# Unsplit fp32 matmuls for the first operands of a two-pass DFT kernel, with another order of its first accumulations

## The chip, the cores and the metric

The kernel runs on one core of one Trainium2 chip. The metric is the device time of one execution in microseconds (us). TensorE (PE) multiplies, VectorE (DVE), ScalarE (ACT) and GpSimd (POOL) work beside it, and SyncE (SP) and POOL each issue transfers from a queue of their own. Inputs lie in HBM.

## What is computed

```python
xn = layernorm(x)                       # x: 2048 x 640
a, b = xn @ hid_re.T, xn @ hid_im.T     # DFT along the hidden dimension
s = seq_re @ a - seq_im @ b             # DFT along the sequence, real part
g = silu(((silu(xn @ w_gate) * (xn @ w_up)) @ w_down))
out = x + s * g
```

Everything is float32. The kernel takes the sequence DFT first (`seq @ xn`), then the hidden one.

## The kernel before, in words

**Precision.** A float32 operand is split into two fp32r parts, `high` and `low`: ACT writes high (L192), DVE writes low = value - high (L197, or L199 where a factor of -1 is folded in). A product is three matmuls, high x high, high x low, low x high (`mm3`, L213 to L215), each 128x128 by 128x512.

**Tiling.** `seq(k)` is called four times (real and imaginary part of the sequence DFT for two halves of its columns). Each call is one level of a Strassen-like scheme with the products p1, d, p5, p2, p6, p3, p7, p4 in this order for k = 0. A product runs over four quarters g = 0..3; a quarter holds two tiles kk of 128 contraction rows. A quarter of p1 has, for each of its tiles, two matmul groups into the banks of p1 and one `direct` group for the last 128 of the 640 columns: 18 matmuls. A quarter of d has the direct group alone (6 matmuls), one of p5, p6, p3 or p7 two groups (12), one of p2 three (18).

**Left operands** come from the DFT matrix `cs`, 128x1024 float32 a quarter (512 KB): Y[g] is block 11, R[g] block 21. `load` (L569) issues them from SP. `accumulate` (L583) adds another block onto the tile in SBUF by a transfer that adds, from POOL: R[g] becomes a21 + a22 after d (`d`, L703), is read by p5, then gets block 11 added (`p5`, L697) and is read by p6 (`p6`, L716). An accumulation must wait until the split that reads the old value is done; the next split waits until it has landed.

**Right operands** are the normalized x. `layer_norm` (L413) works on two tiles of x: DVE statistics (L420, L422), a chain of small operations on DVE (L433 to L437, after a square root on ACT, L432), for tiles 8 to 15 on POOL instead (L441 to L448), and the rows are applied by ACT (L453). Then `right_operand` (L604) splits them, one, two or four tiles at once.

**Order.** `Plan` gives every operation a due time: matmul steps follow each other at 0.226 us a matmul, what they need is due some lead (`LEAD`, L540) before its step, and all operations are sorted by due time (L73). This settles only the order within each engine's and queue's program and where buffers lie; on the chip each engine runs its own list in order, as soon as semaphores allow. Before the first product, 22 matmuls of zeros run (`busy`, L457, called at L1050), and 6 more stand ahead of the third quarter of p1 (L661). The matmuls of p1 and d for k = 0 are interleaved: p1 quarters 0 and 1, d quarter 0, p1 quarter 2, d 1, p1 3, d 2, d 3 (L734).

Of the kernel before, what the change touches and what calls it, by code (L numbers as in the profile page):

```python
# [10 lines left out]
AF = mybir.ActivationFunctionType  # L11
ALU = mybir.AluOpType

P = 128
S, D, F = 2048, 640, 1536
TC = 512
# [121 lines left out]
def tile_fnet_swiglu(  # L138
# [34 lines left out]
    def raw(name, a=0, n=None):  # L173
        o = where[name]
        return raw_arena[:, o + a:o + (pl.size[name][1] if n is None else a + n)]

    def hl(name, i, a=0, n=None):

        key = name, "hl"[i]
        o = where[key]  # L180
        return hl_arena[:, o + a:o + (pl.size[key][1] if n is None else a + n)]


    def split(lead, dst, n, src, reads, a=0, scale=None, sub=0, low_lead=None):


        def like(ap):
            s = src()
            return ap.rearrange("p (a b) -> p a b", b=s.shape[2]) if len(s.shape) == 3 else ap

        def high():
            nc.scalar.activation(like(hl(dst, 0, a, n)), src(), AF.Copy, scale=1.0 if scale is None else scale)  # L192

        def low():
            hi, lo = like(hl(dst, 0, a, n)).bitcast(F32), like(hl(dst, 1, a, n))
            if scale is None:
                nc.vector.tensor_tensor(lo, src(), hi, op=ALU.subtract)  # L197
            else:
                nc.vector.scalar_tensor_tensor(lo, src(), scale, hi, op0=ALU.mult, op1=ALU.subtract)  # L199

        pl.prod(lead, high, reads, [(dst, "h", sub)])
        pl.prod(lead - 2 if low_lead is None else low_lead, low, [*reads, (dst, "h", sub)], [(dst, "l", sub)])

    def both(dst, *subs):
        return [(dst, p, s) for s in (subs or (0,)) for p in "hl"]
# [4 lines left out]
    def mm3(bank, w, m, first, a=0, n=TC):  # L210

        o = ps[:, bank, a:a + n]
        nc.tensor.matmul(o, w(0), m(0), start=first, stop=False, skip_group_check=True)  # L213
        nc.tensor.matmul(o, w(0), m(1), start=False, stop=False, skip_group_check=True)  # L214
        nc.tensor.matmul(o, w(1), m(0), start=False, stop=True, skip_group_check=True)  # L215

    def product(todo, reads):

        banks = sorted({t[0] for t in todo})

        def go():
            for bank, w, m, first in todo:
                mm3(bank, w, m, first)

        pl.step(3 * len(todo), go, reads, [("ps", b) for b in banks])

    def pair(b):
        return ps[:, b[0]:b[0] + len(b), :]
# [276 lines left out]
    def down_operands():  # L505

        for g in range(2):
# [29 lines left out]
    spare = down_operands()  # L537


    LEAD = {("xn", 0): ((2.6, 1.0), (6, 6), (7, 7)), ("xn", 1): ((3.9, 2.0), (4.31, 4.22), (6.2, 4.32)),  # L540
# [10 lines left out]

    def seq(k):
        j, ri = k // 2, k % 2
# [2 lines left out]
        first = {}  # L556
        top, made = {}, set()
        fresh = k == 0

        def is_first(b):  # L560
            f = first.setdefault(b, True)
# [27 lines left out]
                    [(src, 0)], [(dst, 0)])  # L589

        def operand(p, g, name):
            s = pl.buf(("S", k, p, g), "hl", 4 * TC)
            high, low = LEAD.get((p, g), LEAD.get(p, LEAD["S"])) if fresh else LEAD["S"]
            for i, sub in enumerate(halves(p, g)):
                n = 2 * TC // len(halves(p, g))
                lead = (high, low) if n > TC else LEAD["S", i]
                split(lead[0], s, n, lambda i=i, n=n: raw(name, i * n, n), [(name, j) for j in range(2) if n > TC or j == i],
                      i * n, sub=sub, low_lead=lead[1])
            return s

        def halves(p, g):
            return (0, 1) if fresh and (p, g) == ("p1", 0) else (0,)

        def right_operand(p, g, per):  # L604

# [17 lines left out]
        def run(*parts, order=None):  # L623

            todo = []
            start = pl.now
            for i, g in order or [(0, g) for g in range(4)]:  # L630
                p, left, banks, direct = parts[i]
                rights = ([p] if banks else []) + ([f"d{direct[1]}"] if direct else [])
                per = 3 * (len(banks) + (direct is not None))
                at = pl.now
                s = left(g)
                for kk in (2 * g, 2 * g + 1):
                    pl.now = at + kk % 2 * per * MM
                    for r in rights:
                        few = 4 if not fresh or r not in ("p1", "d1", "p2", "d2") else 2 if g > 2 or r[1] == "2" else 1
                        if (r, kk) not in top:  # L640
                            right_operand(r, kk // few, few)
                pl.now = at + 2 * per * MM
                todo.append((p, g, banks, direct, rights, s))
            pl.now = start
            for p, g, banks, direct, rights, s in todo:
                steps = [], []
                reads = [], []
                for kk in (2 * g, 2 * g + 1):
                    i = kk % 2
                    m = lambda part, i=i, s=s: hl(s, part, i * TC, TC)  # L650
# [4 lines left out]
                    subs = halves(p, g)  # L655
                    reads[i].extend(both(s, subs[i % len(subs)]))
                    for r in rights:
                        reads[i].extend(both(*top[r, kk][:2]))
                if fresh and p == "p1":
                    if g == 2:  # L660
                        pl.step(0, lambda: busy(ps[:, b1[0]], 6), [], [("ps", b1[0])])  # L661
                    for step in zip(steps, reads):
                        product(*step)
                else:
                    product(steps[0] + steps[1], list(dict.fromkeys(reads[0] + reads[1])))

        def result(q, b, other, op):
            name = pl.buf(("P", k, q), "raw", len(b) * TC)
# [18 lines left out]
        def p1(g):  # L687
            if not fresh:
                Y[g] = load(11, g, 18)
                return operand("p1", g, Y[g])  # L690
            for i in range(2):
                load_x(2 * g + i, 30 + (3.9 if g == 1 else 0), nc.sync)
            Y[g] = load(11, g, 30) if g else load_tiles(11, (30, 29.8))
            layer_norm(2 * g, 2, *LEAD["xn", g], nc.vector)
            return operand("p1", g, Y[g])
# [7 lines left out]
        def d(g):  # L703
            R[g] = load(21, g, 26 if fresh else 18)
            s = operand("d", g, R[g])
            accumulate(R[g], 22, g, LEAD["d", g][1] - 0.1 if fresh else 7.5)
            return s

        def p2(g):
            if fresh:  # L710
                for kk in (8 + 2 * g, 9 + 2 * g):
                    load_x(kk, (32, 32.7, 31.7, 35.8)[g], nc.gpsimd if g else nc.sync)
                layer_norm(8 + 2 * g, 2, *LEAD["xn", 4 + g], nc.gpsimd)
            return operand("p2", g, load(12, g, 14 if fresh else 17))

        def p6(g):  # L716
            if not fresh:
# [21 lines left out]
            run(first_two[1])  # L739
        if not fresh:  # L740
            product_2()
        run(("p5", p5, b3, None))
        n5 = copy("n5", b3)
        if fresh:
            product_2()
# [346 lines left out]
```

## Time and profile before

| | |
|---|---|
| median of 3 runs | 996.8 us (996.42 to 998.02) |
| the profiled execution | 996.99 us, span 994.6 us from first to last instruction |
| PE, weight loads, DVE, ACT, POOL busy | 99%, 81%, 72%, 50%, 11% |
| mean granted TensorE clock | 0.998 |
| HBM read, written | 145.75 MB, 33.57 MB |

How to read it: PE is busy nearly all the time, so what can be had lies in the moments in which it isn't. The profile names for each wait of an engine the instruction that ended it. A matmul row shows its latency (0.39 us); consecutive ones start 0.227 us apart, and a larger step between two starts is a wait or a slower clock. A row of the timeline may merge equal neighbours: `x3` and the time from the first start to the last end. Queue instructions that issue transfers show only the issue; when data has landed is seen from the engine that waited.

### The profile page before, as it was taken

What the parts mean: (1) busy time and instruction counts of PE and PEld (TensorE: products, weight loads), DVE (VectorE), ACT (ScalarE), POOL (GpSimd) and SP (SyncE); (2) the same over time, 40 slices, a digit from 0 to 9 for tenths busy, and PEclk for the clock granted to TensorE, in tenths of its full rate; (3) what the DMA queues carried; (4) which work ended last, traced back from release to release, by engine and by line L of the source; (5) the groups of instructions that cost most, each with busy time, mean ns of one, the idle gap of its engine ahead of it and who ended that gap; (6) DMA issues with size and microseconds to landing.
All of it is one profiled execution on the core that took longest, in us unless ns stands there. A gap on an engine that the chain in (4) does not pass through costs nothing.

```text
span 994.6 us, 11790 instructions
## 1 busy us (share of the span) xinstructions
PE 982.2 (99%) x4317; PEld 806.2 (81%) x4318; DVE 714.5 (72%) x935; ACT 500.8 (50%) x718; POOL 107.7 (11%) x175
## 2 busy tenths in 40 slices
PE   8999999999999999999999999999999999999998
PEld 5777888888888888888888888888888888887887
DVE  7979767856686686466678886787677666666686
ACT  6676553754375454414655555444334544444342
POOL 1650201011102010001111110000010100000000
PEclk9999999999999999999999999999999999999999
DMA  9779667565756586643535645679950311115683
GB/s 337 213 171 266 225 144 161 209 193 136 179 190 202 134 227 217 216 163 133 186 122 195 229 164 175 205 236 361 323 186 27 106 54 53 53 43 172 230 276 133
DMA packets 71466, 180.10 MB, mean 181 GB/s; under 512 B 6448, under 2 KB 22064, under 8 KB 71408
## 3 DMA queue, kind: packets, MB, share of 16 engines
q1 hardware_dynamic: 57072, 125.71, 38.2%
q0 software_dynamic: 14336, 53.63, 19.5%
q8 instruction: 34, 0.56, 0.2%
q14 instruction: 24, 0.20, 0.1%
HBM read 145.75 MB, written 33.57 MB: 180 GB/s over the span
## 4 chain that ended last, share of the span: by engine, by line
PE 90%; DVE 4%; DMA 3%; ACT 1%; issue 1%; POOL 1%; DVEq 0%; ACTq 0%; POOLq 0%
PE ps L213 30%; PE ps L214 30%; PE ps L215 30%; DMA raw<-in_cs 2%; DVE hl L197 2%; ACT hl L192 1%; DVE bst L420 0%; ACT raw L453 0%; DVE raw L477 0%; DMA raw<-in_x 0%; DVE raw L588 0%; DVE raw L243 0%; POOL raw L585 0%; POOL sm L441 0%; POOL sm L442 0%
## 5 line engine op out<-in xcount | busy, mean ns | idle before, releaser
L213 PE MATMUL ps<-hl 128*128 128x512 f32 (+1 forms) x1430 | 556.7, 389 | 2.9 <-ACT hl L192 2.0
L215 PE MATMUL ps<-hl 128*128 128x512 f32 (+1 forms) x1430 | 556.2, 389 | 2.6 <-DVE hl L197 1.5
L214 PE MATMUL ps<-hl 128*128 128x512 f32 (+1 forms) x1430 | 556.0, 389 | 0.4 <-DVE hl L197 0.4
L192 ACT ACTIVATE hl<-raw 128x1024 fp32r<-128x1024 f32 (+7 forms) x511 | 376.5, 785 | 250.6 <-DVE raw L875 52.5
L197 DVE TENSOR_TENSOR hl<-raw,hl 128x1024 fp32r<-128x1024 f32 (+5 forms) x438 | 395.2, 934 | 131.6 <-ACT hl L192 88.3
L213 PEld LDWEIGHTS ps<-hl 128*128 128x128 f32 x1430 | 268.8, 188 | 60.6 <-ACT hl L192 3.0
L215 PEld LDWEIGHTS ps<-hl 128*128 128x128 f32 x1430 | 268.8, 188 | 59.6 <-DVE hl L197 2.4
L214 PEld LDWEIGHTS ps<-hl 128*128 128x128 f32 x1430 | 268.9, 188 | 56.7 <-DVE hl L197 1.6
L238 ACT ACTIVATE raw<-ps 128x512 f32<-128x512 f32 (+1 forms) x122 | 80.3, 676 | 145.5 <-PE ps L215 107.8
L243 DVE TENSOR_TENSOR raw<-ps,raw 128x512 f32<-128x512 f32 (+1 forms) x90 | 71.6, 796 | 54.2 <-PE ps L215 53.3
L962 DVE TENSOR_TENSOR raw<-raw 128x512 f32<-128x512 f32 x24 | 16.6, 692 | 49.8 <-ACT raw L961 49.8
L199 DVE SCALAR_TENSOR_TENSOR hl<-raw,hl 128x384 fp32r<-128x384 f32 (+5 forms) x73 | 43.8, 601 | 7.8 <-ACT hl L192 4.4
L875 DVE TENSOR_TENSOR raw<-raw 128x256 f32<-128x256 f32 (+1 forms) x96 | 47.8, 519 | 0.0
L585 POOL DMA_DIRECT2D raw<-in_cs x36 | 32.2, 1070 | 128.5 <-DVE raw L588 91.4
L588 DVE TENSOR_TENSOR raw<-raw 128x1024 f32<-128x1024 f32 x28 | 34.1, 1219 | 9.8 <-DMA raw<-in_cs 9.8
L1024 POOL DMA_DIRECT2D out<-raw x10 | 6.7, 673 | 303.1 <-ACT hl L192 245.7
L676 POOL DMA_DIRECT2D p_dram<-raw x24 | 17.2, 760 | 202.3 <-DVE raw L243 153.6
L828 DVE TENSOR_TENSOR raw<-raw 128x1024 f32<-128x1024 f32 (+1 forms) x24 | 24.0, 1040 | 6.4 <-DMA raw<-in_xt 6.4
L940 ACT ACTIVATE raw<-raw 128x512 f32<-128x512 f32 x24 | 15.2, 632 | 23.6 <-DVE raw L243 23.5
L800 POOL DMA_DIRECT2D y_dram<-raw x20 | 10.9, 547 | 132.4 <-ACT raw L238 132.4
L961 ACT ACTIVATE raw<-ps 128x512 f32<-128x512 f32 x24 | 14.3, 596 | 19.7 <-PE ps L215 18.7
L532 POOL DMA_DIRECT2D d_p<-hl x28 | 15.2, 542 | 79.6 <-ACT hl L192 65.5
(45 smaller groups left out, 186.3 us busy)
## 6 DMA issues: line engine op xcount, KB each, us to landing
raw<-in_cs SPq DMA_DIRECT2D x79, 512.0 KB, 5.8
hl<-d_p SPq DMA_DIRECT2D x56, 384.0 KB, 4.1
raw<-in_cs POOLq DMA_DIRECT2D x36, 512.0 KB, 8.9
raw<-in_wb SPq DMA_DIRECT2D x24, 640.0 KB, 4.0
d_p<-hl POOLq DMA_DIRECT2D x28, 384.0 KB, 2.8
raw<-p_dram SPq DMA_DIRECT2D x8, 1280.0 KB, 9.8
p_dram<-raw POOLq DMA_DIRECT2D x16, 512.0 KB, 6.5
raw<-in_hd SPq DMA_DIRECT2D x20, 320.0 KB, 9.0
```

Of the source, the lines that this page charges most:

```text
L192: nc.scalar.activation(like(hl(dst, 0, a, n)), src(), AF.Copy, scale=1.0 if scale is None else scale)
L197: nc.vector.tensor_tensor(lo, src(), hi, op=ALU.subtract)
L199: nc.vector.scalar_tensor_tensor(lo, src(), scale, hi, op0=ALU.mult, op1=ALU.subtract)
L213: nc.tensor.matmul(o, w(0), m(0), start=first, stop=False, skip_group_check=True)
L214: nc.tensor.matmul(o, w(0), m(1), start=False, stop=False, skip_group_check=True)
L215: nc.tensor.matmul(o, w(1), m(0), start=False, stop=True, skip_group_check=True)
L238: pl.post(lambda: nc.scalar.activation(wide(raw(dst, a, n)), pair(b), AF.Copy), pkeys(b), [(dst, a)], after)
L243: pl.post(lambda: nc.vector.tensor_tensor(wide(raw(dst, a, n)), pair(b), wide(raw(other)), op=op), [*pkeys(b), (other, 0)], [(dst, a)], after)
L585: pl.prod(lead, lambda: nc.gpsimd.dma_start(wide(raw(name)), source(q, g), accum_op=ALU.add), [], [(name, 0), (name, 1)], 8)
L588: pl.prod(lead, lambda: nc.vector.tensor_tensor(raw(dst), raw(dst), raw(src), op=ALU.add), [(src, 0)], [(dst, 0)])
L828: pl.prod(46 - 6 * q - 2 * i - half, lambda i=i, op=op, part=part, rows=rows, nb=nb: nc.vector.tensor_tensor(part(), part(), raw(rows, i * ...
L875: pl.prod(lead, lambda o=o, a=a, b=b, op=op: nc.vector.tensor_tensor(o(), a(), b(), op=op), [(w, 0)], [(c, lead)])
```

## The change

- Quarter 0 of p1 and quarters 0 and 1 of d (k = 0) are no longer split. Each of their products is one `nc.tensor.matmul` on float32 operands: 6 in p1 quarter 0, 2 in each of the two d quarters. Since p1 takes minus x, ACT writes a negated copy of 256 columns of tiles 0 and 1 (`negative`). `halves`, which split p1's first operand by tile, goes away.
- The accumulations onto R[0] and R[1] are now planned right behind the d matmuls that read R itself, and wait for these (before, for the low parts).
- The 6 matmuls of zeros ahead of p1's third quarter are removed.
- p5 takes its quarters in the order 0, 2, 3, 1. p6 keeps 0, 1, 2, 3.
- Leads: the rows of tiles 2 and 3 and of tiles 8 to 11 and 14, 15 are applied by other due times; loads of x tiles 10 to 15 and of p2's blocks are due later; the second pair of x tiles is issued behind both halves of p1's first block.

What this makes of each list: POOL's transfers stood before as accumulation on R[0], x 10, 11, accumulation on R[1], x 12 to 15, accumulations on R[2], R[3]; they now stand as R[0], x 10, 11, R[2], R[3], R[1], x 12 to 15. The second round, block 11 onto R, stood as R[0], (small operations for tiles 14, 15), R[1], R[2], R[3]; it now stands as R[0], (the same), R[2], R[3], R[1]. From p3 on the lists of PE, ACT and DVE are the same as before.

```diff
-            for bank, w, m, first in todo:
-                mm3(bank, w, m, first)
-        pl.step(3 * len(todo), go, reads, [("ps", b) for b in banks])
+            for bank, w, m, first, *unsplit in todo:
+                if unsplit:
+                    nc.tensor.matmul(ps[:, bank, :], w(), m(), start=first, stop=True, skip_group_check=True)
+                else:
+                    mm3(bank, w, m, first)
+        pl.step(sum(4 if len(t) > 4 else 3 for t in todo), go, reads, [("ps", b) for b in banks])
...
+        whole = {("p1", 0), ("d", 0), ("d", 1)} if fresh else ()
...
         def operand(p, g, name):
+            if (p, g) in whole:
+                return name
...
-        def halves(p, g):
-            return (0, 1) if fresh and (p, g) == ("p1", 0) else (0,)
+        def negative(kk):
+            name = pl.buf(("neg", kk), "raw", 256)
+            pl.prod(LEAD["neg", kk], lambda: nc.scalar.activation(
+                raw(name).unsqueeze(1), xn_tiles(kk, 1, 0, 256), AF.Copy, scale=-1.0), [(xn, kk, 0)], [(name, 0)])
+            return name
...
+                    if (p, g) in whole:
+                        m = lambda i=i, s=s: raw(s, i * TC, TC)
+                        for e, b in enumerate(banks):
+                            steps[i].append((b, lambda n=top["neg", kk], e=e: raw(n, e * P, P), m, is_first(b), True))
+                        w = lambda kk=kk: xn_tiles(kk, 1, TC, P)[:, 0]
+                        steps[i].append((dbank[direct[0]], w, m, is_first(dbank[direct[0]]), True))
+                        reads[i].extend([(s, i), (xn, kk, 0)] + ([(top["neg", kk], 0)] if banks else []))
+                        continue
...
-                    if g == 2:
-                        pl.step(0, lambda: busy(ps[:, b1[0]], 6), [], [("ps", b1[0])])
...
+                if p == "d" and (p, g) in whole:
+                    accumulate(R[g], 22, g, 0)
...
-                load_x(2 * g + i, 30 + (3.9 if g == 1 else 0), nc.sync)
+                load_x(2 * g + i, 30 + (5.2 if g == 1 else 0), nc.sync)
...
-            accumulate(R[g], 22, g, LEAD["d", g][1] - 0.1 if fresh else 7.5)
+            if ("d", g) not in whole:
+                accumulate(R[g], 22, g, LEAD["d", g][1] - 0.1 if fresh else 7.5)
...
-                    load_x(kk, (32, 32.7, 31.7, 35.8)[g], nc.gpsimd if g else nc.sync)
+                    load_x(kk, (32, 27.5, 25.4, 29.4)[g], nc.gpsimd if g else nc.sync)
...
-            return operand("p2", g, load(12, g, 14 if fresh else 17))
+            return operand("p2", g, load(12, g, 11 if fresh else 17))
...
-        run(("p5", p5, b3, None))
+        run(("p5", p5, b3, None), order=((0, 0), (0, 2), (0, 3), (0, 1)) if fresh else None)
```

More of the change, by code (lines that the diff above doesn't have):

```diff
@@ L537, in tile_fnet_swiglu @@
     spare = down_operands()
-    LEAD = {("xn", 0): ((2.6, 1.0), (6, 6), (7, 7)), ("xn", 1): ((3.9, 2.0), (4.31, 4.22), (6.2, 4.32)),
[6 rows of a table removed]
+    LEAD = {("xn", 0): ((2.6, 1.0), (6, 6), (7, 7)), ("xn", 1): ((4.1, 3.1), (6.4, 6.3), (7.5, 6.5)),
+            ("xn", 2): ((3.9, 3), (5, 4.5), (6.8, 6.1)), ("xn", 3): ((3.9, 3), (6.87, 6.7), (9.8, 7.9)), ("xn", 4): ((11, 11), (17, 17), (17.1, 17.1)),
+            ("xn", 5): ((10, 10), (18.1, 18.1), (18.2, 18.2)), ("xn", 6): ((7.5, 7.5), (15.7, 15.7), (15.8, 15.8)),
+            ("xn", 7): ((7.5, 7.5), (15.4, 15.4), (15.5, 15.5)), ("neg", 0): 1.8, ("neg", 1): 2.6,
[1 row of a table added]
             ("Tp1", 4): (0, 3.8, 2.6), ("Td1", 4): (0, 3.7, 2.55), ("Tp1", 5): (0, 4.9, 3.5), ("Td1", 5): (0, 4.8, 3.4),
[3 rows of a table removed]
[4 rows of a table added]
     def seq(k):
@@ L591, in operand @@
         def operand(p, g, name):
+            if (p, g) in whole:
+                return name
             s = pl.buf(("S", k, p, g), "hl", 4 * TC)
             high, low = LEAD.get((p, g), LEAD.get(p, LEAD["S"])) if fresh else LEAD["S"]
[L594 to L598, printed above, removed]
-            return s
-        def halves(p, g):
-            return (0, 1) if fresh and (p, g) == ("p1", 0) else (0,)
+            split(high, s, 2 * TC, lambda: raw(name), [(name, 0), (name, 1)], low_lead=low)
+            return s
+        def negative(kk):
[3 more added lines that the diff above has]
+            return name
         def right_operand(p, g, per):
@@ L632, in run @@
                 rights = ([p] if banks else []) + ([f"d{direct[1]}"] if direct else [])
-                per = 3 * (len(banks) + (direct is not None))
+                per = (4 if (p, g) in whole else 3) * (len(banks) + (direct is not None))
                 at = pl.now
@@ L637, in run @@
                     pl.now = at + kk % 2 * per * MM
+                    if (p, g) in whole:
+                        if p == "p1":
+                            top["neg", kk] = negative(kk)
+                        continue
                     for r in rights:
@@ L649, in run @@
                     i = kk % 2
+                    if (p, g) in whole:
+                        m = lambda i=i, s=s: raw(s, i * TC, TC)
[4 more added lines that the diff above has]
+                        reads[i].extend([(s, i), (xn, kk, 0)] + ([(top["neg", kk], 0)] if banks else []))
+                        continue
                     m = lambda part, i=i, s=s: hl(s, part, i * TC, TC)
@@ L654, in run @@
                         steps[i].append((dbank[direct[0]], tw(rights[-1], kk, 0), m, is_first(dbank[direct[0]])))
-                    subs = halves(p, g)
-                    reads[i].extend(both(s, subs[i % len(subs)]))
+                    reads[i].extend(both(s))
                     for r in rights:
```

14 rows, old and new, of the table LEAD are left out of this document.

## The prediction, made before the changed kernel ran

> **What bounds the kernel now.** The page first, then stretches of the span, then PE's starts in order of time.
>
> ```profile
> PE 982.2 (99%) x4317; PEld 806.2 (81%) x4318; DVE 714.5 (72%) x935; ACT 500.8 (50%) x718; POOL 107.7 (11%) x175
> ```
> ```profile
> 9.00:107.00 98.00, 92.91 (x391) 73.02 (x390) 88.10 (x134) 67.10 (x87) 32.66 (x53) 0.98 0.85 253
> 107.00:986.00 879.00, 878.19 (x3880) 726.76 (x3880) 619.40 (x784) 428.79 (x623) 74.23 (x115) 1.00 0.55 173
> ```
>
> From 107 us on PE misses 0.8 us in 879: there only matmuls count, 0.2265 us each (879/3880), and the change leaves them alone. (Buffers are placed anew, so that a write may meet another reader; the 0.8 us bounds such waits as they are now, and I take none.) Everything it can win or lose lies in the first 107 us, and it counts only if the last wait there, at 107 us, ends earlier or later. PE's waits:
>
> ```profile
> 12.82 0.50 PE L215 MATMUL ps<-hl 128*128 128x512 f32 x1 [0.70 <-DVE hl L199]
> ...
> 20.25 1.24 PE L460 MATMUL ps<-z 128*128 128x512 bf16 x5
> 22.17 0.50 PE L213 MATMUL ps<-hl 128*128 128x512 f32 x1 [0.68 <-ACT hl L192]
> ...
> 29.32 0.50 PE L213 MATMUL ps<-hl 128*128 128x512 f32 x1 [1.37 <-ACT hl L192]
> 29.67 0.40 PE L214 MATMUL ps<-hl 128*128 128x512 f32 x1
> 30.41 0.65 PE L215 MATMUL ps<-hl 128*128 128x512 f32 x1 [0.35 <-DVE hl L199]
> ...
> 51.80 0.50 PE L215 MATMUL ps<-hl 128*128 128x512 f32 x1 [1.37 <-DVE hl L197]
> 52.15 0.40 PE L213 MATMUL ps<-hl 128*128 128x512 f32 x1
> ...
> 85.21 0.50 PE L214 MATMUL ps<-hl 128*128 128x512 f32 x1 [0.39 <-DVE hl L197]
> ...
> 107.17 0.50 PE L213 MATMUL ps<-hl 128*128 128x512 f32 x1
> ```
>
> PE waits for splits, late because DVE and ACT are full (DVE 90% of this stretch), and behind them for the accumulations. The chain of waits has two long transfers, each followed by the split that needs it:
>
> ```profile
> 32.13 11.47 DMA raw<-in_cs
> 43.69 1.07 ACT hl L192
> ...
> 59.43 13.11 DMA raw<-in_cs
> 72.62 1.07 ACT hl L192
> ```
>
> The first is the last of the a22 accumulations, the second (issued 59.43, landed 72.54) the third of POOL's seven in a row:
>
> ```profile
> 58.26 6.26 POOL L585 DMA_DIRECT2D raw<-in_cs  x7 [0.28 <-ACT hl L192]
> ```
>
> **The change part by part.**
>
> *Unsplit matmuls.* No row shows one. Three matmuls leave out low x low, so four passes of 0.2265, 0.91 us, is my value: ten products, +2.3 us of PE. Bounds from the nearest rows: one pass each, -4.5 us in all; four passes at the slow clock's 0.43 us (below), +10.4. The Trainium skill, "FP8 and Floating Point Precision", section TensorE Precision Notes, gives true FP32 four passes; by that the sum is the same +2.3.
>
> *Splits removed.* Durations, grouped by form:
>
> ```profile
> L197 DVE TENSOR_TENSOR hl<-raw,hl 128x1024 fp32r<-128x1024 f32 x18 | 21.4, 1218 | 3.0 <-ACT hl L192 2.9
> L197 DVE TENSOR_TENSOR hl<-raw,hl 128x512 fp32r<-128x512 f32 x5 | 3.4, 678 | 0.2 <-ACT hl L192 0.2
> L199 DVE SCALAR_TENSOR_TENSOR hl<-raw,hl 128x256 fp32r<-128x256 f32 x6 | 2.4, 396 | 0.4 <-ACT hl L192 0.4
> L197 DVE TENSOR_TENSOR hl<-raw,hl 128x128 fp32r<-128x128 f32 x6 | 1.7, 284 | 0.0
> L192 ACT ACTIVATE hl<-raw 128x256 fp32r<-128x256 f32 x10 | 4.1, 412 | 0.2
> ```
>
> DVE loses two each of these four: 2 x (1.22 + 0.68 + 0.40 + 0.28) = 5.2 us. ACT loses the same high parts and gains two negations of 0.41. First product: tile 0's rows are applied as now,
>
> ```profile
> 7.29 0.92 ACT L453 ACTIVATE raw<-raw,sm,rowst 128x640 f32<-128x640 f32 x1 [0.50 <-DVE sm L437]
> ```
>
> so it is negated by 8.6, and the zeros end at 9.0: no new wait. The second pair of x tiles is issued one slot later; DVE has no split ahead of their statistics any more, which covers it. The earlier due times of rows cost nothing: ACT works 67 of these 98 us.
>
> *Zeros removed.* The wait of 20.25 to 22.17 was for tile 4's rows and splits; the DVE chain behind them ended at 20.7, three subtractions and one sum stood ahead of quarter 3's splits:
>
> ```profile
> 20.55 0.16 DVE L437 SCALAR_TENSOR_TENSOR sm<-mv,rowst 128x2 f32<-128x2 f32 x1
> ...
> 25.12 3.50 DVE L197 TENSOR_TENSOR hl<-raw,hl 128x1024 fp32r<-128x1024 f32 x3
> 28.54 1.22 DVE L477 TENSOR_TENSOR raw<-raw 128x1024 f32<-128x1024 f32 x1
> 29.67 0.69 DVE L199 SCALAR_TENSOR_TENSOR hl<-raw,hl 128x512 fp32r<-128x512 f32 x1
> ```
>
> Laid end to end in the new order, DVE has: statistics of tile 3 to 10.4, chain for 2, 3 to 11.6, p1 quarter 1 low (after its high) 12.0 to 13.2, tile 2 lows (after ACT) 14.0 to 14.6, statistics 4 to 15.7, tile 3 lows to 16.2, statistics 5 to 17.3, quarter 2 low to 18.4, chain for 4, 5 to 19.3: 1.4 us sooner, and tile 4's high part is there at 20.4 + 0.3. PE arrives at 9.0 + 6 x 0.91 + 18 x 0.2265 + 2 x 0.91 = 20.3: the wait shrinks to some 0.3. Quarter 2 and d 1 take it to 26.5. Quarter 3's low part comes after two subtractions instead of three, all 1.4 sooner: 2 x 1.15 + 1.2 + 0.7 from 23.8 is 28.0, where it was 30.4, and no slow clock follows a wait this short. So p5 begins at 28.0 + 28 x 0.2265 = 34.3; it began 20 slots after 33.85 (below), at 38.4.
>
> *Accumulations of a22.* R[0]'s now waits for PE's d 0 (20.3); x 10 and 11 queue behind it, uncritical. R[1]'s waits for d 1, but stands behind R[3]'s anyway. The four x tiles that stood ahead of the last two now follow: 4 x 320 KB at 405 GB/s is 3.2 us,
>
> ```profile
> 34.00:36.00 2.00, 2.00 (x11) 1.63 (x10) 1.93 (x7) 0.32 (x1) 0.00 (x0) 1.00 1.00 405
> ```
>
> and d's splits come about 1.5 us sooner. The last landing, at 43.6 in the chain, moves to about 38.9. p5's quarter 3 then meets its low part at about 40.8 (DVE has statistics between), 1 us of wait, and the last two quarters, p2 (72 matmuls) and p6's quarter 0 (12) follow without one: 40.8 + 108 x 0.2265 = 65.2. Before, p6 quarter 0 ended at 52.15 + 81 x 0.2265 = 70.5. The order 0, 2, 3, 1 does its work: **PE leads by 5.3 us** here.
>
> *Block 11 onto R, where the lead goes.* p6 still takes quarter 1 second, but R[1]'s accumulation is now third of POOL's row. When does that row begin? Behind POOL's small operations for tiles 14 and 15, which need DVE's statistics. In the new order DVE finishes R[1]'s low part at 38.9 + 1.06 + 0.9 + 1.2 = 42.0, then statistics 2.2, p2's splits 1.2 and 1.1, statistics 2.2: 48.5. POOL's eight operations took, by pair of tiles:
>
> ```profile
> 41.20:47.00 5.80, 5.15 (x8) 1.00 0.07 13
> 48.10:52.20 4.10, 3.52 (x8) 1.00 0.01 2
> ```
>
> Long beside DVE's back-to-back subtractions (three at 42.29 to 46.0), short between. Behind these statistics stands a run of subtractions again: 5.7 us, so the row begins at 54.3, 4.0 us before today's 58.26. Landings of the first three today, from what ACT waited for, and DVE behind them:
>
> ```profile
> 63.82 1.06 ACT L192 ACTIVATE hl<-raw 128x1024 fp32r<-128x1024 f32 x1 [0.22 <-DMA raw<-in_cs]
> 68.77 2.01 ACT L192 ACTIVATE hl<-raw 128x1024 fp32r<-128x1024 f32 x2 [3.90 <-DMA raw<-in_cs]
> ```
> ```profile
> 69.87 1.23 DVE L197 TENSOR_TENSOR hl<-raw,hl 128x1024 fp32r<-128x1024 f32 x1 [3.54 <-ACT hl L192]
> ```
>
> R[1] as third lands 72.54 - 58.26 = 14.3 after the row's start: 68.6. **PE stands from 65.2 to 69.7**, and to 70.9 for the low part. Behind that split on ACT and DVE queue quarters 2 and 3, whose data is there, and everything of p3.
>
> *What ends last.* DVE makes p6's quarter 1 low at 69.7 and quarter 2 low at 70.9; that one starts at 69.87 today. From there DVE's list is today's, nearly without a gap, down to the combination that frees PE's bank at 107.17:
>
> ```profile
> 105.90 1.22 DVE L243 TENSOR_TENSOR raw<-ps,raw 128x1024 f32<-128x1024 f32 x1
> ```
>
> So 36.0 us later again: 107.17 + 1.0. PE's own count agrees: quarter 1 at 70.9 against 70.7, plus a slow-clock window (1.7), less today's waits at 81.8, 85.2 and 107.2 (1.3): +0.6. The sum is **+1.0 us** on the profiled execution's 996.99 (span 994.6 and 2.4 around it): 998.0. The median of the runs is 0.2 below that execution, so 997.8.
>
> **The rivals.**
>
> *The lead survives.* If R[1]'s second accumulation lands by 64, PE keeps its 5.3 us at p6 and DVE's list gives up to 4.0 (the row's earlier start): 996.8 - 4.3 = 992.5. For it: 4 to 5 us less DVE work is real. Against: R[1] would have to land 10 us after its row starts, as second does today (68.77 - 58.26 = 10.5), and it is third.
>
> *It lands half-way.* POOL's pair takes 4.1 instead of 5.7, and p3's loads from SP, which share the queue's time with the first two, come later: 1.6 + 1 us sooner, 995.2.
>
> *The clock: slower.* Today's wait of 27.8 to 29.3 halves the clock afterwards:
>
> ```profile
> 30.00:32.00 2.00, 1.65 (x5) 1.30 (x5) 2.00 (x4) 2.00 (x3) 0.62 (x1) 0.65 1.07 316
> 32.00:34.00 2.00, 2.00 (x6) 1.51 (x6) 2.00 (x2) 0.42 (x1) 0.87 (x1) 0.50 1.05 272
> 33.42 0.63 PE L213 MATMUL ps<-hl 128*128 128x512 f32 x1
> 33.85 0.47 PE L214 MATMUL ps<-hl 128*128 128x512 f32 x1
> ```
>
> Eight matmuls 0.43 apart, 1.6 us lost. The new wait is three times as long. If it slows two such stretches once PE runs again, PE's count passes DVE's: +0.6 + 1.7 = +2.3, and with R[1] a microsecond later +3.3: 1000.1. It decides as soon as more than one stretch is slow behind 70.9. The Trainium skill, "TensorE: Matmul & The Clock Gate", section HAM oscillation, warns only of idle gaps over about 3.4 us; the trace is stricter, 1.5 and 0.5 us were enough, and by the page too the new gap of 4.5 is long enough. An unsplit product of 1.6 us instead of 0.91 would make PE 7 us later, use up the lead, and end near the same 1000.
>
> *The change does not do what it says* finds no support: the new lists hold the ten single matmuls, the negations and the transfers in the order told.
>
> **How the numbers follow.** About 0.2% (2 us) is what a measurement of this kernel can tell from none: faster is below 994.8, slower above 998.8. Forecast, 997.8 (996.0 to 999.3): 0.50. Half-way, 995.2: 0.17. Lead kept, 992.5: 0.13. Slow clock or dear matmuls, 1000.1: 0.20. Faster: 0.13 and 0.07 of half-way, 0.20. Slower: 0.20 and 0.12 of the forecast's upper end, 0.32. The range, 994.0 to 1000.4, leaves out the kept lead and a little on the other side.
>
> **What would show it.** The new page should have PE's longest wait near 65 to 70 us, ended by ACT L192 behind a transfer, a granted clock of about 0.5 soon after, no half clock near 31, PE's waits before p5 under 2 us in all, unsplit rows 0.91 us apart. Wrong, if POOL's row of seven begins before 52, if p6's second quarter starts before 67, or if PE is late at p6 (unsplit matmuls far from 0.91).

## The result, and the profile after

| | before | after |
|---|---|---|
| median of 22 runs each, in turn on the same chips | 996.8 us (996.36 to 998.02) | 998.8 us (997.49 to 1001.14) |
| the profiled execution, its span | 996.99, 994.6 us | 998.95, 997.0 us |

The ratio after : before is 1.0021, with a 95% interval of 1.0014 to 1.0028: 2.0 us slower. The forecast was 997.8.

First the page's line of busy times and two stretches of the changed kernel; columns of the stretches are length, PE, PEld, DVE, ACT, POOL busy, granted clock, DMA share, GB/s.

```profile
PE 982.7 (99%) x4302; PEld 804.2 (81%) x4302; DVE 710.5 (71%) x927; ACT 496.8 (50%) x712; POOL 106.2 (11%) x175
```
```profile
9.00:107.00 98.00, 91.07 (x363) 69.07 (x363) 83.42 (x128) 62.32 (x81) 31.29 (x53) 0.97 0.78 228
107.00:986.00 879.00, 878.25 (x3881) 726.69 (x3880) 620.22 (x783) 429.53 (x624) 73.35 (x114) 1.00 0.55 176
```

Behind 107 us nothing has changed (0.75 us without PE, 0.8 before). In the first 98 us DVE does 4.7 us less (83.42 for 88.10) and ACT 4.8 less, and still PE's missing time rises from 5.1 to 6.9 us. PE's starts in order of time; the number in brackets is the wait just before, with what ended it.

```profile
8.76 2.84 PE L224 MATMUL ps<-raw 128*128 128x512 f32 x6 [0.16 <-ACT raw L606]
12.07 2.84 PE L224 MATMUL ps<-raw 128*128 128x512 f32 x6 [0.47 <-ACT raw L606]
14.95 0.50 PE L213 MATMUL ps<-hl 128*128 128x512 f32 x1
...
21.54 0.50 PE L213 MATMUL ps<-hl 128*128 128x512 f32 x1 [0.46 <-ACT hl L192]
...
25.76 1.88 PE L224 MATMUL ps<-raw 128*128 128x512 f32 x4
27.74 0.50 PE L213 MATMUL ps<-hl 128*128 128x512 f32 x1
...
28.65 0.50 PE L215 MATMUL ps<-hl 128*128 128x512 f32 x1 [0.17 <-DVE hl L199]
...
65.22 0.39 PE L215 MATMUL ps<-hl 128*128 128x512 f32 x1
70.76 0.79 PE L213 MATMUL ps<-hl 128*128 128x512 f32 x1 [5.15 <-ACT hl L192]
72.02 0.79 PE L214 MATMUL ps<-hl 128*128 128x512 f32 x1 [0.47 <-DVE hl L197]
72.61 0.63 PE L215 MATMUL ps<-hl 128*128 128x512 f32 x1
...
76.45 0.57 PE L215 MATMUL ps<-hl 128*128 128x512 f32 x1
76.86 0.40 PE L213 MATMUL ps<-hl 128*128 128x512 f32 x1
```

Up to p5 the change does what it should: waits of 0.16, 0.47, 0.46 and 0.17 us (before: 0.70, the one at 20.3, 1.37, 0.35), and p6's first quarter ends at 65.2 instead of 70.5. Then all of that lead goes in one wait of 5.15 us. POOL's row of seven, ACT's split that had to wait for it, and DVE's splits behind that:

```profile
54.47 6.25 POOL L589 DMA_DIRECT2D raw<-in_cs  x7 [0.29 <-ACT hl L192]
```
```profile
69.65 3.90 ACT L192 ACTIVATE hl<-raw 128x1024 fp32r<-128x1024 f32 x4 [9.88 <-DMA raw<-in_cs]
```
```profile
70.74 2.36 DVE L197 TENSOR_TENSOR hl<-raw,hl 128x1024 fp32r<-128x1024 f32 x2 [9.37 <-ACT hl L192]
...
107.44 1.22 DVE L246 TENSOR_TENSOR raw<-ps,raw 128x1024 f32<-128x1024 f32 x1
```

R[1] is the third of the row. It lands 15.2 us behind the row's start (54.47 to 69.65), while R[2] and R[3] lie there already: the one split that ACT makes at 69.65 is followed by three more without a gap. After the wait the granted clock is half:

```profile
66.00:68.00 2.00, 0.00 (x0) 0.00 (x0) 0.00 (x0) 0.00 (x0) 0.00 (x0) 1.00 1.03 279
70.00:72.00 2.00, 0.79 (x1) 0.29 (x1) 1.26 (x2) 2.00 (x3) 0.00 (x0) 0.50 1.05 207
72.00:74.00 2.00, 1.98 (x5) 1.60 (x6) 2.00 (x2) 1.54 (x2) 0.00 (x0) 0.50 1.08 213
74.00:76.00 2.00, 2.00 (x6) 1.54 (x5) 2.00 (x3) 1.06 (x1) 0.00 (x0) 0.50 1.07 211
76.00:78.00 2.00, 2.00 (x8) 1.60 (x7) 2.00 (x3) 0.00 (x0) 0.00 (x0) 0.80 1.01 219
```

From 72.02 to 76.86 eleven matmuls start (0.43 apart); at 0.2265 they would need 2.5 us, so 2.3 us are lost, where the forecast had counted one stretch of 1.7. From 76.86 to beyond 107 PE has no wait at all: the three waits of before (at 81.8, 85.2 and 107.2) are gone, and the DVE combination (L246, before L243) that freed PE's bank at 107.17 starts at 107.44 instead of 105.90 and no longer holds anyone up. The same instruction's last use in the run tells the whole difference; below it is for before and for after:

```profile
L243 DVE TENSOR_TENSOR raw<-ps,raw x90: 681/692/1225, 77.1 to 977.9; 128x512 f32<-128x512 f32 x72, 128x1024 f32<-128x1024 f32 x18
```
```profile
L246 DVE TENSOR_TENSOR raw<-ps,raw x90: 681/692/1225, 78.7 to 980.4; 128x512 f32<-128x512 f32 x72, 128x1024 f32<-128x1024 f32 x18
```

The last starts 2.5 us later (977.9, 980.4); the spans differ by 2.4.

### The profile page after: what moved, and what is told of

It reads as the page before. It is cut to its first block, busy times and chain, and to the rows that moved or that the text cites. A ratio compares the mean times of both kernels' runs of the same rounds, so it can differ in the third digit from the quotient of the medians.

```text
span 997.0 us, 11726 instructions
## 1 busy us (share of the span) xinstructions
PE 982.7 (99%) x4302; PEld 804.2 (81%) x4302; DVE 710.5 (71%) x927; ACT 496.8 (50%) x712; POOL 106.2 (11%) x175
## 5 line engine op out<-in xcount | busy, mean ns | idle before, releaser
L213 PE MATMUL ps<-hl 128*128 128x512 f32 x1420 | 553.0, 389 | 6.5 <-ACT hl L192 5.6
L214 PE MATMUL ps<-hl 128*128 128x512 f32 x1420 | 552.5, 389 | 0.5 <-DVE hl L197 0.5
L215 PE MATMUL ps<-hl 128*128 128x512 f32 x1420 | 552.2, 389 | 0.2 <-DVE hl L199 0.2
L192 ACT ACTIVATE hl<-raw 128x1024 fp32r<-128x1024 f32 (+6 forms) x503 | 372.0, 788 | 270.7 <-PE ps L214 61.6
L246 DVE TENSOR_TENSOR raw<-ps,raw 128x512 f32<-128x512 f32 (+1 forms) x90 | 71.5, 796 | 58.7 <-PE ps L215 57.6
L958 ACT ACTIVATE raw<-raw 128x512 f32<-128x512 f32 x24 | 15.2, 632 | 22.9 <-DVE raw L246 22.9
```

The source lines that it names most:

```text
L246: pl.post(lambda: nc.vector.tensor_tensor(wide(raw(dst, a, n)), pair(b), wide(raw(other)), op=op), [*pkeys(b), (other, 0)], [(dst, a)], after)
```

## The experiments

Theory: the row lands the quarters in the order 2, 3, 1 and p6 asks for 1, 2, 3; that eats the lead, and the stand costs the clock besides. Rivals: the unsplit matmuls themselves cost the time; only the clock does; or DVE's list sets the end whatever PE does. Each kernel ran 4 to 11 times and was timed against the kernel before on its own chip; "us" is the difference of the medians. Profiles are of one execution each.

| kernel | median | against before | ratio, 95% interval |
|---|---|---|---|
| p6_order | 995.5 | -1.4 us | 0.9985, 0.9976 to 0.9994 |
| p6_zeros | 998.5 | +1.6 | 1.0014, 1.0005 to 1.0022 |
| p5_natural | 1002.2 | +5.3 | 1.0055, 1.0042 to 1.0068 |
| before_p5order | 1006.1 | +9.2 | 1.0090, 1.0076 to 1.0103 |
| row_swapped | 994.9 | -2.1 | 0.9974, 0.9964 to 0.9985 |
| row_earlier | 995.7 | -1.3 | 0.9984, 0.9975 to 0.9993 |
| p1_unsplit_only | 1001.8 | +4.8 | 1.0044, 1.0031 to 1.0056 |
| before_both_orders | 1000.2 | +3.2 | 1.0031, 1.0019 to 1.0042 |
| r1_early | 994.7 | -2.4 | 0.9974, 0.9965 to 0.9983 |
| r1_early_y_late | 995.4 | -1.7 | 0.9981, 0.9971 to 0.9990 |
| p3_loads_behind | 999.7 | +2.2 | 1.0024, 1.0013 to 1.0034 |
| r0_r1_early | 992.8 | -4.7 | 0.9956, 0.9944 to 0.9968 |

### p6_order: let p6 ask in the order of landing

```diff
-        run(("p6", p6, b2, None))
+        run(("p6", p6, b2, None), order=((0, 0), (0, 2), (0, 3), (0, 1)) if fresh else None)
```

> The changed kernel, with the fourth product of the path (p6) also taking its quarters in the order 0, 2, 3, 1, the order in which the row of accumulations lands them (59.8, 66.2, 69.6 in the changed kernel's trace). Theory (the lead of 5.3 us is eaten because p6 asks second for the quarter that lands third): PE goes on at 65.2 with quarter 2 instead of standing 5.15 us, stands twice for 1 to 2 us, has the last quarter's low part at about 72 and ends p6 some 5 us sooner; the gain in the total is what the VectorE list behind it allows: its last low part of p6 comes at about 72 instead of 74.3, so 2.3 us less, 996.5, with 994 to 997.5 as bounds (PE's whole 5 us; only the two slow windows). Rival one (the unsplit matmuls and the later chains are the cost, the order of p6 does not matter): 998.8 as the changed kernel, within 0.5. Rival two (the stand only matters by the clock): 1.5 us less, 997.3, with the granted clock at 1.00 through 65 to 77.

995.5: faster than before, 3.3 us below the changed kernel and 1.0 below the likeliest value of the theory. The profile of p6_order, its waits near 60 and the stretch from 9 to 107:

```profile
59.34 0.50 PE L213 MATMUL ps<-hl 128*128 128x512 f32 x1 [0.92 <-ACT hl L192]
60.01 0.49 PE L214 MATMUL ps<-hl 128*128 128x512 f32 x1 [0.16 <-DVE hl L197]
61.74 0.50 PE L215 MATMUL ps<-hl 128*128 128x512 f32 x1 [1.24 <-DVE hl L197]
```
```profile
9.00:107.00 98.00, 94.20 (x385) 71.12 (x384) 87.38 (x132) 66.67 (x87) 32.11 (x55) 1.00 0.82 241
```

PE is busy 3.1 us more in these 98 us (94.20 for 91.07), the clock is whole in this execution. The three waits are not in p6: they lie in p2's last quarter, which begins at 59.34, and p6, from 65.5 on, runs without one. So the theory's two waits in p6 did not come, and 2.3 us of others did, ahead of it. The first rival falls: the unsplit matmuls are all still there. The second does not fit either, since it gave at most 1.5 us.

### row_swapped: let the row land in p6's order

```diff
-                accumulate(R[g], 11, g, -6)
+                accumulate(R[g], 11, g, (-6, -6, -11.6, -9)[g])
```

> The changed kernel with p6's quarters as they are (0, 1, 2, 3) and POOL's row reordered instead: block 11 goes onto R[1] second, then onto R[2] and R[3], by due times alone. Theory (what costs is that the row's order and p6's order disagree): R[1] lands when R[2] did, near 60, its low part is there at about 62, PE does not stand at 65.2 and the half clock of 70 to 77 is gone. As with p6's order changed, 995.5, between 994.5 and 996.5. Rival (p6's other order brought its 3.3 us by something else, such as the order of splits or the third product's operands): 998.8 within 0.5.

994.9, as the theory said, with p6 as in the changed kernel. On PE nothing waits between 41.8 and 70; on ACT of row_swapped R[1]'s split comes at 62, R[2]'s at 68:

```profile
61.99 1.06 ACT L192 ACTIVATE hl<-raw 128x1024 fp32r<-128x1024 f32 x1 [1.57 <-DMA raw<-in_cs]
68.03 2.00 ACT L192 ACTIVATE hl<-raw 128x1024 fp32r<-128x1024 f32 x2 [4.99 <-DMA raw<-in_cs]
```

p6_order besides sends SP's first load for p3 3.3 us later (60.03 for 56.75), row_swapped does not (56.89). Two edits that share nothing but the agreement of the two orders take away the same loss. That the disagreement causes it is shown.

### p6_zeros: keep the wait, take the idle away

```diff
+                    if fresh and (p, g) == ("p6", 1):
+                        pl.step(0, lambda: busy(ps[:, b3[0]], 20), [], [("ps", b3[0])])
```

The zeros overwrite one of the two banks in which p5's sum stands, onto which p3 adds: half of that block of the result lacks p5's share here.

> The changed kernel with 20 bf16 matmuls of zeros (about 4.5 us, into a bank that is free then) ahead of p6's second quarter, inside the 5.15 us in which PE stands at 65.2 to 70.8: the wait for data stays, only the idle goes. Theory: the two half-clock windows of 70.0 to 76.8 go; PE's matmuls run at 0.2265 us instead of 0.43, so PE is some 2.5 us ahead of the changed kernel at 77, and the rest meets VectorE's list, which is 1 us later than before's: total 1 to 1.5 us less, 997.5. Rival one (VectorE's list alone sets the end, PE's slow windows are hidden): no change, 998.8 within 0.4. Rival two (PE alone sets it): the whole 2.5 us less, 996.3.

998.5, 0.4 us below the changed kernel, and the intervals of the two overlap: a difference is not shown, the gain of 1 to 1.5 us that the theory gave did not come, and the time is the one of rival one. In the profile of p6_zeros the clock stays whole, and yet PE waits for the bank again:

```profile
70.00:72.00 2.00, 0.74 (x3) 0.26 (x2) 1.35 (x2) 2.00 (x3) 0.00 (x0) 1.00 1.04 205
72.00:74.00 2.00, 2.00 (x9) 1.63 (x10) 2.00 (x2) 1.47 (x2) 0.00 (x0) 1.00 1.09 215
```
```profile
107.34 1.22 DVE L246 TENSOR_TENSOR raw<-ps,raw 128x1024 f32<-128x1024 f32 x1
```
```profile
108.13 0.39 PE L215 MATMUL ps<-hl 128*128 128x512 f32 x1
108.61 0.50 PE L213 MATMUL ps<-hl 128*128 128x512 f32 x1
```

The matmul that started at 107.17 before starts at 108.61, when the combination of 107.34 is done: DVE's list alone is worth +1.4 us. That is the forecast's step "36.0 us later again", which had +1.0. In the changed kernel PE came past even that, by the clock: the last L246 lies at 980.4 there and here at

```profile
L246 DVE TENSOR_TENSOR raw<-ps,raw x90: 680/691/1225, 78.6 to 979.5; 128x512 f32<-128x512 f32 x72, 128x1024 f32<-128x1024 f32 x18
```

so in this pair of profiled executions the slow clock adds 0.9 us to what DVE's list costs anyway; the medians have 0.4 for it, which is not clear of noise. The third rival is thus right about the path of most of the loss, but not about its cause: what makes DVE's list late is again the order. The L246 that starts at 107.44 in the changed kernel starts at 103.16 in p6_order and at 104.69 in row_swapped.

### p5_natural, before_p5order, before_both_orders: the parts apart

```diff
-        run(("p5", p5, b3, None), order=((0, 0), (0, 2), (0, 3), (0, 1)) if fresh else None)
+        run(("p5", p5, b3, None))
```

> The changed kernel with p5's quarters in the order 0, 1, 2, 3 again, unsplit products, due times and everything else of the change kept. Theory: p5's second quarter now asks for R[1], whose first accumulation lands last of the four (39.2); its low part is there at about 42, so PE stands about 5 us at 37 and loses up to two slow windows (3 us) more; against that R[1]'s second accumulation goes second in POOL's row and p6 does not stand. PE is at p6's second quarter at about 70 to 73: total between 998 and 1002, likeliest 1000. Rival (the order is what costs; without it the rest of the change keeps its 4 us): 995 or less.

before_p5order puts that line the other way round into the kernel before, and nothing else; before_both_orders has p6's new order (the diff of p6_order) besides.

> The kernel before with nothing but p5's order 0, 2, 3, 1. Theory: without the earlier landings p5 gains nothing from the order, while p6's second quarter finds its accumulation third in the row: in before's trace the second landed at 68.8, the third at 72.5, so PE stands some 4 us at p6 and loses one or two slow windows (1.6 us each): 4 to 7 us slower than before, 1001 to 1004. Rival (the unsplit matmuls cost the 2 us, the order is harmless): 996.8 within 0.5.

> The kernel before with the order 0, 2, 3, 1 in p5 and in p6 and nothing else of the change. Theory: p6's stand of the run with p5's order alone (1006.1) goes, some 3 to 5 us, but p5 still asks third for R[3], whose first accumulation lands last at 43.6 in before's queue order, and the splits that the unsplit products remove are still there: 1001 to 1003.5, slower than before. Rival (the two orders do everything and the unsplit products nothing): 995.5 as p6_order.

1002.2, 1006.1 and 1000.2: the first just above the range that the theory gave, the second 2 us above it, the third 0.8 below. All three are slower than before, as it said, and no rival is near. p5_natural's waits in p5, then those of before_p5order in p5 and p6:

```profile
41.46 0.50 PE L213 MATMUL ps<-hl 128*128 128x512 f32 x1 [3.02 <-ACT hl L192]
42.72 0.50 PE L214 MATMUL ps<-hl 128*128 128x512 f32 x1 [0.76 <-DVE hl L197]
```
```profile
42.33 0.76 PE L213 MATMUL ps<-hl 128*128 128x512 f32 x1 [2.61 <-ACT hl L192]
...
46.71 0.79 PE L215 MATMUL ps<-hl 128*128 128x512 f32 x1 [2.33 <-DVE hl L197]
...
78.12 0.50 PE L213 MATMUL ps<-hl 128*128 128x512 f32 x1 [1.60 <-ACT hl L192]
```

In before's queue order R[2] and R[3] are the late ones, so p5's order 0, 2, 3, 1 hurts there, and the stand halves the clock for long:

```profile
44.00:46.00 2.00, 0.39 (x1) 0.00 (x0) 1.93 (x6) 2.00 (x3) 0.34 (x1) 0.50 0.00 0
48.00:50.00 2.00, 2.00 (x6) 1.52 (x6) 1.97 (x5) 1.97 (x4) 1.64 (x6) 0.50 0.00 0
```

That stand in p5, at 42 to 53, is what my expectation of before_p5order had left out. With p6's order put right the kernel before still loses 3.2 us, which is p5's part; the other 6.0 of the 9.2 go with p6's order and are inside the 4 to 7 that I had for p6 alone. In shares: with both products in the order of landing, the rest of the change (unsplit products, removed zeros, due times) is worth 4.6 us (+3.2 to -1.4); p6's order is worth 3.4 in the changed kernel and 6.0 in the one before. So what the change does besides the orders is a gain, though these runs do not tell its three parts apart, and its order of p5 needs p6 to go along.

### p1_unsplit_only: the d pairs split again

From p6_order:

```diff
-        whole = {("p1", 0), ("d", 0), ("d", 1)} if fresh else ()
+        whole = {("p1", 0)} if fresh else ()
...
-            ("d", 2): (8.7, 8.4), ("d", 3): (7.8, 6.8)}
+            ("d", 0): (4.95, 4.85), ("d", 1): (5.5, 5.1), ("d", 2): (8.7, 8.4), ("d", 3): (7.8, 6.8)}
```

> p6_order's kernel with a21's two pairs split again (the four unsplit d products become twelve matmuls: 0.9 us less of PE, 2 x (1.05 ACT + 1.22 DVE) and the first tiles' small splits more). Theory (the unsplit products pay because they take splits off VectorE ahead of p1's third and fourth quarters): those quarters' low parts come 2 to 3.5 us later, R[1]'s first accumulation stands in another place of the queue, and p5 begins 2 to 3 us later: 997.3 to 999, likeliest 998. Rival (the d pairs could as well stay split; only PE's count matters): 994.6 to 995.5.

1001.8, 6.3 us above p6_order and 2.8 above the upper end of what the theory gave. In p1_unsplit_only ACT applies tile 4's rows late, after DVE's chain, and PE stands:

```profile
21.75 0.92 ACT L456 ACTIVATE raw<-raw,sm,rowst 128x640 f32<-128x640 f32 x1 [1.66 <-DVE sm L440]
```
```profile
22.92 0.50 PE L213 MATMUL ps<-hl 128*128 128x512 f32 x1 [3.09 <-ACT hl L192]
```

with the clock halved after it (0.65 and 0.50 at 24 to 28). DVE's chain for tiles 4 and 5 ends at 21.7 us, behind the splits that came back, where it ends at 19.3 in p6_order. The due times were made for the unsplit d, so part of the 6.3 us may be had back by others; that was not tried. What the run shows is that PE's own count (0.9 us less here) does not decide; that the loss comes from splits ahead of DVE's statistics fits the trace, but how much of it is theirs and how much the due times' is not shown.

### p3_loads_behind: why 15.2 us and not 14.3

```diff
-            add(R[g], load(12, g, 17), 12)
+            add(R[g], load(12, g, 17, nc.gpsimd if fresh and g in (1, 2) else nc.sync), 12)
```

(`load` takes the queue as an argument.)

> The changed kernel, natural order of p6, with the loads of block 12 for p3's second and third quarters taken from SP's queue (issued at 57, among the row's transfers) and put on POOL's, as sixth and eighth behind the row's first five. Question: why R[1] landed 15.2 us after the row's start and not the 14.3 that before's third needed. Theory (SP's two loads share the DMA engines with the row): R[1] lands 1 to 2.5 us sooner, at 12.7 to 14.2 behind the row's start, and PE's stand of 5.15 us shrinks by as much; the time is open from 996.5 to 999.5, because p3's second sum then gets its load at about 75 and VectorE may wait there. Rival (the row's adding transfers are slow by themselves): R[1] lands 15 us behind the row's start, and the time is 998.8 or worse.

In p3_loads_behind the row starts at 54.79 and R[1]'s split at 66.97:

```profile
54.79 2.73 POOL L589 DMA_DIRECT2D raw<-in_cs  x3 [0.29 <-ACT hl L192]
```
```profile
66.97 2.95 ACT L192 ACTIVATE hl<-raw 128x1024 fp32r<-128x1024 f32 x3 [6.88 <-DMA raw<-in_cs]
```

12.2 us instead of 15.2, so 3.0 sooner, beyond the 1 to 2.5 that I expected. So the row's landing time is not a constant of the row: SP's loads for p3, which go out at 57 in the changed kernel, cost R[1] 3 us. But they do not explain the question itself. Before and after, the first of them goes out 2.3 us behind the row's start (58.26 and 54.47):

```profile
60.57 0.33 SPq L572 DMA_DIRECT2D raw<-in_cs  x1
```
```profile
56.75 0.33 SPq L576 DMA_DIRECT2D raw<-in_cs  x1
```

Why before's third lost only 2.1 of the 3 us, with the same loads at the same distance, stays open. The total did not gain (999.7): PE stood 2.14 at p6, but DVE then waited for the loads, and PE for DVE:

```profile
84.19 0.50 PE L214 MATMUL ps<-hl 128*128 128x512 f32 x1 [2.07 <-DVE hl L197]
```

### row_earlier, r1_early, r1_early_y_late, r0_r1_early: is there more?

row_earlier, from p6_order; then r1_early, from row_swapped; then r1_early_y_late and r0_r1_early, both from r1_early:

```diff
-                accumulate(R[g], 11, g, -6)
+                accumulate(R[g], 11, g, -4.9 if g == 2 else -6)
...
-                accumulate(R[g], 11, g, (-6, -6, -11.6, -9)[g])
+                accumulate(R[g], 11, g, (-6, 1.5, -11.6, -9)[g])
...
-            accumulate(Y[g], 21, g, 11.5)
+            accumulate(Y[g], 21, g, -6 if fresh and g > 1 else 11.5)
...
-                accumulate(R[g], 11, g, (-6, 1.5, -11.6, -9)[g])
+                accumulate(R[g], 11, g, (-3.2, 1.5, -11.6, -9)[g])
```

> The changed kernel with p6's quarters in the order 0, 2, 3, 1 and, besides, R[2]'s accumulation of block 11 issued ahead of POOL's small operations for tiles 14 and 15 (at about 49 instead of 54). In p6_order's trace PE still waits 0.9 and 1.24 us near 60 to 62 for R[0] and R[2]; R[2] was issued at 54 and had to share with the transfers behind it. Theory: R[2] lands some 4 us sooner, the wait of 1.24 us goes, the others move up by one transfer, and VectorE, which then has its list ready sooner, follows: 0.9 to 1.5 us less than p6_order, 994.2. Rival (what binds then is VectorE's list, waiting for p3's loads at 71): 995.5 as p6_order, within 0.4.

> row_swapped's kernel with R[1]'s accumulation of block 11 issued ahead of POOL's small operations for tiles 14 and 15 (near 50 instead of 56). In row_swapped's trace VectorE stands 4.82 us at 64.3 to 69.1 for R[2], which lands near 68 as second of the row; from there its list has no gap to 103 and PE waits 2.9 us for it between 66 and 84. Theory (that list binds, and its start is the landing of R[2]): R[2] lands a transfer sooner, 3 to 5 us, VectorE starts sooner by as much, and PE's 2.9 us go except where p3's loads are late (in row_earlier's trace they held VectorE for 1.5 us at 71): 992.5 to 994, likeliest 993.3. Rival (POOL's pair for tiles 14 and 15, pushed back by 0.9 us, holds up the splits of p2's last quarter as it did in row_earlier, or p3's loads bind): 994.9 as row_swapped, within 0.4.

> r1_early's kernel with the last two of the four accumulations onto Y (block 21) issued behind the store of p2's result (near 76) instead of in POOL's row at 56 to 62. Between 60 and 84 the DMA queues of all these kernels are busy 1.03 to 1.07 of the time, and p3's loads share them with Y's accumulations, which nobody reads before the seventh product at about 84. Theory: p3's loads land up to 5 us sooner (two adding transfers of about 2.6 us less ahead of them), VectorE's waits for them go, and PE's remaining waits with them: 0.5 to 2 us less than r1_early. Rival (the transfers behind the store come too late for the seventh product, which then waits): 1 to 3 us more than r1_early. A third way, no difference within 0.4, would say that p3's loads do not bind.

> r1_early's kernel with R[0]'s accumulation of block 11 issued one pair of tiles earlier too (ahead of POOL's small operations for tiles 12 and 13). In r1_early's trace PE waits 0.46 and 0.47 us near 60 for p2's last splits, whose rows for tile 15 were pushed back by the 0.9 us of R[1]'s issue. Theory: with R[0] moved up the pair 14, 15 is back where row_swapped had it, these two waits go: 0.5 to 0.9 us less than r1_early, 994.0. Rival (POOL's pair starts behind VectorE's statistics, so an earlier issue frees nothing, or the pair 12, 13 is pushed back instead): 994.7 within 0.4.

row_earlier gained nothing. PE's waits of 0.93, 0.16 and 1.24 us are still there at 60 to 63, though R[2] went out 4 us sooner: I had taken the wrong cause from p6_order's trace. In row_earlier's list ACT's splits for p2's last quarter stand behind a sum on DVE that needs tile 15's rows:

```profile
57.30 1.23 DVE L480 TENSOR_TENSOR raw<-raw 128x1024 f32<-128x1024 f32 x1 [3.35 <-ACT raw L456]
```
```profile
58.56 5.67 ACT L192 ACTIVATE hl<-raw 128x1024 fp32r<-128x1024 f32 x7 [1.29 <-DVE raw L480]
```

r1_early is 0.2 us below row_swapped, no difference that the intervals show, where I had expected 1.6: its rival's time. r1_early_y_late is 0.7 above r1_early, on the side of its rival though less than it gave, and the intervals overlap. The theory's gain did not come. In its trace the rival's wait is there: ACT's splits for the seventh product now wait for Y, DVE for them, and PE for DVE's combination at 106,

```profile
91.05 2.96 ACT L192 ACTIVATE hl<-raw 128x1024 fp32r<-128x1024 f32 x3 [2.25 <-DMA raw<-in_cs]
```
```profile
106.05 0.50 PE L213 MATMUL ps<-hl 128*128 128x512 f32 x1 [1.86 <-DVE raw L246]
```

r0_r1_early has the lowest median of the study, 992.8, 4.7 us below before and 6.0 below the changed one; it was expected at 994.0. Its profiled execution (994.9) was the second slowest of its six, which go from 991.9 to 995.3, and in it the two waits that I meant to remove are still there (0.39 and 0.46). So the time is measured, and its cause isn't.

## Why the prediction came out as it did

The forecast of 997.8 lay 1.0 us below the median, half of the measured 2.0 us. The mechanism held; two terms were too small, and some agreements on the way are luck. By its own steps:

- *What bounds the kernel*: held. Nothing changed behind 107 us.
- *Unsplit matmuls*, four passes, 0.91 us each: the three from 12.07 to 14.95 took 0.96 each, the two from 25.76 to 27.74 0.99, with the change of kind at their ends. +2.8 instead of +2.3. The Trainium skill, "FP8 and Floating Point Precision", section TensorE Precision Notes, has four passes for true FP32; these rows agree.
- *Splits removed, zeros removed*: right in kind. PE's waits ahead of p5 came to 1.3 us, and there was no half clock near 31. The negations of tiles 0 and 1 cost 0.16 and 0.47 us that the step had at nothing; quarter 2 of p1 came 0.9 late, and p5 began at 35.2 instead of 34.3.
- *Accumulations of a22*: the last landing was forecast for 38.9 and its split ran at 39.26; p6's first quarter began its last matmul at 65.2, where the forecast had its end. Part of that is luck: p5 began 0.9 us late, and then waited 0.2 us for R[3]'s low part instead of 1.
- *Block 11 onto R, where the lead goes*: the mechanism held, and row_swapped and p6_order show it from both sides. The row began at 54.47 (forecast 54.3; the terms written there add up to 48.7, not 48.5, and so to 54.4), again with luck: POOL's pair took 4.5 us instead of 5.7 (49.70 to 54.18), but the issue for R[0], which the step did not count, took 1.0 ahead of it (48.66 to 49.63).
- **The mis-sized term: R[1]'s landing**, "14.3 after the row's start", measured 15.2. I had carried before's distance over as a fixed length of the row, though I had named p3's loads as sharing the queue; they are worth 3 us of it (p3_loads_behind), but they stood at the same distance in before, so where the 0.9 us come from is open. PE stood to 70.8 and, for the low part, to 72.0, for 69.7 and 70.9.
- *What ends last*: DVE's list, +1.0, is +1.4 with the clock kept whole (p6_zeros). In the changed kernel the low part of p6's quarter 2 started at 71.88, 2.0 us behind before's 69.87, and L246 only 1.5 later than before (107.44 for 105.90): "36.0 us later again" came to 35.6.
- **The second: the clock**, "plus a slow-clock window (1.7)". The clock was half from 70.0 to 76.8, two windows of the length of before's one (30.4 to 33.9), with 2.3 us lost at PE, so that PE and not DVE set the end. That is the rival *The clock: slower*, with both of its conditions (R[1] a microsecond later, a second window), and it gave 1000.1. It was right in its mechanism; its price was too high by about 1 us, because it took two windows at 1.7 each, while in the first 2 us of half clock (70.0 to 72.0) PE, standing for the low part, started a single matmul and had little to lose.

The rival *The lead survives*, which did not come, took off 4.3 us where its own terms give DVE's list at most 4.0.

So in the profiled spans +1.0 became +1.4 on DVE's path and, by the clock, +2.4 on PE's; what lies around the span came to 2.0 us instead of the 2.4 that the sum took from before, which brings the execution back to +2.0. In the medians the changed kernel has +2.0 and p6_zeros +1.6, so how much the clock adds is shown only by the pair of traces. That PE and DVE reached 107 us within a microsecond of each other is why so many different losses come to so little, and why one loss removed gives back only its excess over the next.

## What to carry to other kernels

When a product's quarters are reordered, follow the same buffers to their next use: here the order in which p5 released R set the order in which its next values landed, and the product after it still asked in the old one. A lead won upstream counts only up to the first wait that it doesn't reach; find that wait, and what feeds it, before adding up instructions saved. A transfer's time from issue to landing is not a constant that can be carried over: ask what else is in flight.

## What the runs showed of the hardware

Short waits can halve the clock, and not each time. In row_earlier the waits of 0.93, 0.16 and 1.24 us, all within 3.4 us, were followed by half clock:

```profile
62.00:64.00 2.00, 1.41 (x3) 1.17 (x4) 2.00 (x4) 2.00 (x3) 0.00 (x0) 0.53 1.08 205
64.00:66.00 2.00, 2.00 (x7) 1.60 (x6) 2.00 (x3) 1.29 (x2) 0.00 (x0) 0.61 1.02 217
```

In p6_order's profile the same three (0.92, 0.16, 1.24) were not: its clock is 1.00 from 9 to 107. Executions of one kernel differ in this too: of p6_order's eleven, five have a mean granted clock of 1.000 and took 994.0 to 995.3 us, the profiled one (994.06) among them; six have 0.996 to 0.998 and took 995.5 to 996.8. What decides between them the runs don't tell. The Trainium skill, "TensorE: Matmul & The Clock Gate", section HAM oscillation, names idle gaps above about 3.4 us as the cause; here 2.3 us in three pieces were enough once.

Transfers that add moved 207 to 213 GB/s with the DMA engines full (share 1.05 to 1.08, 70 to 76 us of the changed kernel), where a stretch of mainly plain loads from the same queue moved 405 (34 to 36 us before).
